# Adding the second bias of a feed-forward block on VectorE instead of TensorE, in a one-core training step

## The chip, the cores and the metric

The kernel runs on one core of one Trainium2 chip. The metric is device time in microseconds (us) of one execution; shorter is better. A core has five engines that run their own instruction streams: TensorE (PE in the profile; PEld is its weight load), VectorE (DVE), ScalarE (ACT), GpSimd (POOL) and SyncE (SP). SP, ACT and POOL issue DMA transfers from queues. Engines wait for each other by semaphores, and each works through its own stream in order.

## The reference

The reference is one transformer layer, forward and backward, on 2048 tokens of width 512 in bf16. The forward part is cut to what matters here:

```
def _B_ref(x, w1, b1, w2, b2):
    h = jnp.einsum("bsd,df->bsf", x, w1) + b1
    h = _gelu(h)
    return jnp.einsum("bsf,fd->bsd", h, w2) + b2

h  = x + _A_ref(_layernorm(x), A_wqkv, A_wo)        # sliding, dilated attention of 32 heads
h2 = h + _B_ref(_layernorm(h), B_w1, B_b1, B_w2, B_b2)
```

with F = 1792 hidden features. The outputs are h2 and the gradients of x, wqkv, wo, w1, b1, w2 and b2 for a given gradient of h2. The change concerns the term b2 in h2. It is one row of 512 numbers, added to each of the 2048 tokens.

## The kernel before, in words

The tokens are cut into NC = 4 chunks of CH = 512; a chunk is TPC = 4 token tiles of P = 128 rows. The kernel has three stages.

In the first stage, to about 150 us, `p1_round` does layer norm, the projections and the attention chunk by chunk. Its step `p1_d` leaves the residual h of a chunk in `h_all[c]`, a bf16 tile of 128 x 4 x 512 that stays on chip.

The second stage, the feed-forward block with its gradient, reaches to about 380 us. Two generators are interleaved by hand. `p2_h(c)` makes hidden activations of a chunk in four blocks of features: matmuls into `ps_h` (L583), two ACT evictions to `xb` and `xa` (L584, L585), a sigmoid on ACT (L590), and eight VectorE operations (L588 to L596) that end in `gt`, the gelu, and `dt`, its derivative. `p2_rest(c)` then does, for each of four token tiles, the product with w2 into `ps_f2` (shown in the profile as ps_f): 14 matmuls (L615), one matmul of a row of ones with the row `b2row` (L616), and one with the identity that adds the residual (L617). ACT copies the sum to `h2s` (L619) and stores it (L620). After that come the gradient products `ps_gg` (L628, multiplied into `dt` by VectorE at L630) and `ps_gl2` (L639), then the layer norm's gradient. While chunk c is in `p2_rest`, chunk c + 1 is in `p2_h`.

PSUM tiles rotate: `ps_h` has four buffers, `ps_f2` shares two with other tiles. `xb` and `xa` have two buffers each.

In these two stages a scheduler sets each engine's order of instructions from the program's dependences; the order of the code is only where it starts from. At the start of the second stage SP issues transposing loads of w2 and w1 (`w2T`, `w1T`) and of the gradient (`goT`), and transposes of `gt` and `dt` through `tst`, with POOL storing the results.

The third stage, from about 380 us, has its order written out by hand (`tc.manual_schedule()`): attention gradients on VectorE with weight gradients filled in on TensorE.

Of the kernel before, what the change touches and what calls it, by code (L numbers as in the profile page):

```python
# [10 lines left out]
P = 128  # L11
BF16 = mybir.dt.bfloat16
F32 = mybir.dt.float32
ACT = mybir.ActivationFunctionType
ALU = mybir.AluOpType
# [12 lines left out]
def _ap(apobj, dims, off=0):  # L28
    return bass.AP(tensor=apobj.tensor, offset=apobj.offset + off, ap=[list(d) for d in dims])
# [7 lines left out]
def kernel(  # L37
# [21 lines left out]
    V, A, T, G, SY = nc.vector, nc.scalar, nc.tensor, nc.gpsimd, nc.sync  # L59
# [4 lines left out]
    S, D = xf.shape  # L64
# [4 lines left out]
    TPC = CH // P  # L69
# [16 lines left out]
    def LP(name, side="left"):  # L86
        p = pool(name, 1, side)
        pools.append(p)
        return p

    const = LP("const")
# [8 lines left out]
    def Y(name):  # L100
        return psY.tile([P, 512], F32, name=name, tag="y")

    def TT(name):
        return psT.tile([P, 1024], BF16, name=name, tag="t")
# [9 lines left out]
    ind8 = const.tile([P, 8], BF16, name="ind8")  # L114
    Emat = const.tile([P, 4, 32], BF16, name="Emat")
    mk = const.tile([16, 2, 4, 32], BF16, name="mk")
    ones_row = const.tile([1, P], BF16, name="ones_row")
    ones_col = const.tile([P, 1], BF16, name="ones_col")
    mhalf = const.tile([P, TPC], F32, name="mhalf")
    zrow = const.tile([18, D], BF16, name="zrow")  # L120
    rowi = const.tile([P, 2], mybir.dt.uint32, name="rowi")
    V.memset(ones_row[:], 1.0)
    V.memset(mhalf[:], -0.5)
    V.memset(zrow[:], 0.0)
    rstd1 = const.tile([P, NT], F32, name="rstd1")
    rstd2 = const.tile([P, NT], F32, name="rstd2")
    b1b = const.tile([FT, P], BF16, name="b1b")
    b2row = const.tile([1, D], BF16, name="b2row")
    b1c = const.tile([P, FT], F32, name="b1c")
    gb1p = const.tile([P, FT, NC], F32, name="gb1p")  # L130

# [22 lines left out]
    def load_rows(t, src, c):  # L154
        SY.dma_start(out=t[:], in_=src[c * CH:(c + 1) * CH, :].rearrange("(j p) d -> p j d", p=P))
# [168 lines left out]
    h_all = []  # L324

    def p1_ln(c):
        xp, xg = ((wff, "w20"), (wff, "w28"), (early, "xt"), (late, "xt"))[c]
        xt = xp.tile([P, TPC, D], BF16, name="xt", tag=xg, bufs=1)
        load_rows(xt, xf, c)
        if c == 0:  # L330
            for i in range(3):
                o = (1, 0, 2)[i] * D
                SY.dma_start(out=wqkv[:, :, o:o + D], in_=A_wqkv[:, o:o + D].rearrange("(a p) j -> p a j", p=P))
        ln1 = early.tile([P, TPC, D], BF16, name="ln1", tag="ln1", bufs=2)
        layernorm(early, xt, rstd1, c, ln1)
        store_rows(ln1_d, c, ln1)
        ln1T = early.tile([P, DC, CH], BF16, name="ln1T", tag="ln1T", bufs=2)
        to_fm(ln1, ln1T)
        st_[c].update(xt=xt, ln1T=ln1T)
# [24 lines left out]
    def p1_v(c):  # L364
        vt = early.tile([P, 4, PAD + CH], BF16, name="vt", tag="vt", bufs=1)
        p1_proj(c, 2, vt, PAD)
        to_tm_store(early, vt, PAD, v_d, c, True)
        G.dma_start(out=vf_d[:, :, PAD + c * CH:PAD + (c + 1) * CH], in_=vt[:, :, PAD:PAD + CH])

    def p1_tm(c):  # L370
        to_tm_store(early, st_[c]["kt"], PAD, k_d, c, True)
        to_tm_store(early, st_[c]["qt"], 0, q_d, c, False)

    def p1_dots(c):
        d = st_[c]
        d["L"] = [X("ps_L") for _ in range(2)]
        dots(late, d["qt"], d["kt"], d["L"], c == 0)
# [57 lines left out]
    def p1_d(c):  # L435
        d = st_[c]
        oT, xt = d["oT"], d["xt"]
        ht = htile(f"h{c}")
        for j in range(TPC):
            ps = X("ps_wo")  # L440
            for k in range(DC):
                T.matmul(ps[:], lhsT=oT[:, k, j * P:(j + 1) * P], rhs=wo[:, k, :], start=(k == 0), stop=False)
            T.matmul(ps[:], lhsT=ident[:], rhs=xt[:, j, :], start=False, stop=True)
            A.copy(out=ht[:, j, :], in_=ps[:])
        h_all.append(ht)
        ln2 = late.tile([P, TPC, D], BF16, name="ln2", tag="ln2", bufs=1)
        layernorm(late, ht, rstd2, c, ln2)
        store_rows(ln2_d, c, ln2)
        d["ln2"] = ln2

    def p1_d2(c):
        to_fm(st_[c]["ln2"], ln2T[c])
# [34 lines left out]
    def p1_round(c):  # L487
        if c + 2 < NC:
            p1_ln(c + 2)
        if c == 0:  # L490
            for (d_t, r) in ((v_d[0], 0), (k_d[0], 0), (q_d[NC - 1], CH), (go_d[NC - 1], CH)):
                SY.dma_start(out=d_t[r:r + RPAD, :], in_=zrow[:])
            SY.dma_start(out=b1b[:], in_=B_b1.rearrange("(f p) -> f p", p=P))
            SY.dma_start(out=b2row[:], in_=B_b2.rearrange("(a n) -> a n", a=1))
        if c + 1 < NC:
            p1_dots(c + 1)
        if c > 0:
            p1_d(c - 1)
        if c == NC - 2:
            p1_v(c + 1)  # L500
        if c > 0:
            p1_d2(c - 1)
        if c + 2 < NC:
            p1_qk(c + 2)
        if c + 1 < NC:
            p1_sm1(c + 1)
        p1_o(c, 0)
        if c == NC - 1:
            return
        if c < NC - 2:  # L510
            p1_v(c + 1)
        p1_sm2(c + 1)
        p1_o(c, 1)
        p1_tm(c + 1)
        if c == 1:
            w2.extend(wparts(wff, "w2", W3, True))
            for a_, b_, t_ in w2:
                G.dma_start(out=t_[:], in_=B_w2[a_ * P:b_ * P, :].rearrange("(a p) d -> p a d", p=P))
        if c == 0:
            pb = TT("pb1")  # L520
            T.transpose(pb[:, 0:FT], b1b[:], ident[0:FT, 0:FT])
            V.tensor_copy(out=b1c[:], in_=pb[:, 0:FT])
# [14 lines left out]
    def load_wT(name, src):  # L537
# [3 lines left out]
    NS = 5  # L541
    SA = 2
    FFT = dict(goT=([P, DC, CH], 1), tst=([P, 16, P], 3), gout=([P, TPC, D], 1), ln2r=([P, TPC, D], 1),
               h2s=([P, D], 2), gyr=([P, D], 2), junk=([P, D], 1), u=([P, D], 2), 
               xb=([P, 4, PAD + CH], 2), xa=([P, 2, 4, 512], 2))

    ffp = {}
# [1 line left out]
    def ft(tag, name=None):  # L549
        shp, nb = FFT[tag]  # L550
        pl = ffA if tag in ("xb", "xa", "tst") else ffp["B"]
        return pl.tile(shp, BF16, name=name or tag, tag=tag, bufs=nb)
# [49 lines left out]
    def p2_rest(c):  # L602
        d = ps2[c]
        gts, dts = d["g"], d["d"]
        goT = goT0.pop() if c == 0 else ft("goT")
        if c > 0:
            SY.dma_start_transpose(out=goT[:], in_=gof[c * CH:(c + 1) * CH, :])
        gout = ft("gout")
        load_rows(gout, gof, c)
        ln2 = ft("ln2r")  # L610
        load_rows(ln2, ln2_d, c)
        for j in range(TPC):
            ps = psT.tile([P, 512], F32, name="ps_f2", tag="t")
            for f in range(FT):
                T.matmul(ps[:], lhsT=gts[f // 4][:, f % 4, j * P:(j + 1) * P], rhs=wrow(w2, f), start=(f == 0), stop=False)  # L615
            T.matmul(ps[:], lhsT=ones_row[:], rhs=b2row[:], start=False, stop=False)  # L616
            T.matmul(ps[:], lhsT=ident[:], rhs=h_all[c][:, j, :], start=False, stop=True)  # L617
            h2s = ft("h2s")
            A.copy(out=h2s[:], in_=ps[:])  # L619
            A.dma_start(out=h2f[c * CH + j * P:c * CH + (j + 1) * P, :], in_=h2s[:])  # L620
            yield
        for bi, (f0, f1) in enumerate(FB):
            for fp in range(f0, f1, 2):
                for i in range(2):
                    f = fp + i
                    ps = Y("ps_gg")
                    for dc in range(DC):
                        T.matmul(ps[:], lhsT=wcol(w2T, dc, f), rhs=goT[:, dc, :], start=(dc == 0), stop=(dc == DC - 1))  # L628
                    dsl = dts[bi][:, f - f0, :]
                    V.tensor_tensor_reduce(out=dsl, in0=ps[:], in1=dsl, scale=1.0, scalar=0.0,  # L630
                                           op0=ALU.mult, op1=ALU.add, accum_out=gb1p[:, f, c:c + 1])
                yield
            tok_store(dts[bi], f0, f1, ghT_d, c)
        gh = htile(f"gh{c}")
        gh_all[c] = gh
        for j in range(TPC):
            ps = psT.tile([P, 512], F32, name="ps_gl2", tag="t")
            for f in range(FT):
                T.matmul(ps[:], lhsT=dts[f // 4][:, f % 4, j * P:(j + 1) * P], rhs=wrow(w1T, f),  # L639
                         start=(f == 0), stop=(f == FT - 1))  # L640
            t = c * TPC + j
            ln_bwd(ffp["B"], ps[:], ln2[:, j, :], rstd2[:, t:t + 1], gout[:, j, :], gh[:, j, :])
            yield
# [82 lines left out]
    w1T = wparts(wfb, "w1T", W4, True)  # L726
    for a_, b_, t_ in w2T:
        SY.dma_start_transpose(out=t_[:], in_=B_w2[a_ * P:b_ * P, :])
    goT0 = [ft("goT")]
    SY.dma_start_transpose(out=goT0[0][:], in_=gof[0:CH, :])  # L730
    for a_, b_, t_ in w1T:
# [506 lines left out]
```

## Time and profile before

| | before |
|---|---|
| time, median of 5 runs | 666.92 us (664.36 to 672.56) |
| profiled execution: time | 665.72 us |
| profiled execution: span of the engines | 663.8 us |
| TensorE busy | 609.6 us, 3948 matmuls |
| VectorE busy | 512.9 us, 758 instructions |
| ACT busy | 367.4 us, 570 instructions |
| granted TensorE clock, mean | 0.992 |

The span is the time from the first to the last instruction of the profiled execution; the time around it is 1.9 us more. Busy time is the sum over an engine's instructions, overlaps counted once. In a timeline the first two numbers are start and duration in us; a bracket at the end tells how long the engine sat idle before, and what ended the wait. In a table of groups, the numbers behind the bar are busy us, mean ns of one, and idle us before them. L616 is line 616 of the kernel before.

### The profile page before, as it was taken

Reading aid. Unit: us, or ns where it says so; the run is one execution under the profiler, and the core shown is the slowest. Engines: PE = TensorE matmul, PEld = TensorE weight load, DVE = VectorE, ACT = ScalarE, POOL = GpSimd, SP = SyncE. Lnnn points to the kernel's source line nnn. Section 1 sums busy time; section 2 is a strip of 40 time slices with the busy share of each in tenths; the row PEclk is TensorE's granted clock in tenths of the full one; section 3 lists DMA queues with packets and bytes.
Section 4 is the critical chain, followed back from the end, with each engine's and each line's share of the span. In section 5 each row is a group of like instructions: output and inputs, shape, how many; then the busy total and the mean of one; then the engine's idle time right before and its main releaser. Section 6 shows DMA issues by size and latency. Waiting matters only on the chain. (4 is left out here: it accounts for less than half of the span.)

```text
span 663.8 us, 10258 instructions
## 1 busy us (share of the span) xinstructions
PE 609.6 (92%) x3948; PEld 285.5 (43%) x3948; DVE 512.9 (77%) x758; ACT 367.4 (55%) x570; POOL 161.1 (24%) x183
## 2 busy tenths in 40 slices
PE   3888989877899999999999899999999999989997
PEld 1343434332444344444344434434456566433443
DVE  7989989969879869859839797987987898296400
ACT  2588877788583645556331362863494356464311
POOL 3341635431001110110100234430323134030100
PEclk9999999898899999999999999999999999999999
DMA  8583848744999997987995989996899689979141
GB/s 257 193 301 119 295 138 305 225 153 105 241 223 274 238 219 170 219 223 180 257 252 162 247 315 349 368 321 234 281 403 327 218 283 356 299 247 319 50 158 48
DMA packets 147806, 158.87 MB, mean 239 GB/s; under 512 B 94461, under 2 KB 132398, under 8 KB 141102
## 3 DMA queue, kind: packets, MB, share of 16 engines
q1 hardware_dynamic: 120078, 69.58, 40.2%
q0 software_dynamic: 15376, 77.63, 34.0%
q10 hardware_dynamic: 12304, 11.01, 5.2%
q8 instruction: 31, 0.51, 0.3%
q14 instruction: 17, 0.14, 0.1%
HBM read 87.63 MB, written 48.03 MB: 204 GB/s over the span
## 5 line engine op out<-in xcount | busy, mean ns | idle before, releaser
L1021 DVE TENSOR_TENSOR prb<-R,cf 128x2048 bf16<-128x2048 bf16 x96 | 110.8, 1218 | 11.3 <-DMA R<-go_d,rowi 4.2
L188 ACT ACTIVATE gyr<-ps_gl,rstd 128x512 bf16<-128x512 f32 x32 | 21.9, 687 | 77.9 <-PE ps_gl L1084 32.0
L583 PE MATMUL ps_h<-ln2T,w 128*128 128x512 bf16 x224 | 56.9, 384 | 1.4 <-ACT xa L585 1.0
L913 PE MATMUL ps_gw<-gwm,ln_r 128*128 128x256 bf16 x448 | 53.1, 273 | 2.0 <-ACT gwst L832 1.0
L628 PE MATMUL ps_gg<-goT,w2T 128*128 128x512 bf16 x224 | 54.6, 378 | 0.3 <-DVE gb1p L630 0.3
L639 PE MATMUL ps_gl<-w1T,dt 128*128 128x512 bf16 x224 | 52.3, 379 | 1.6 <-ACT gyr L188 1.3
L905 PE MATMUL ps_gw<-gout_r,gwm 128*128 128x512 bf16 x224 | 53.1, 380 | 0.0
L615 PE MATMUL ps_f<-w,gt 128*128 128x512 bf16 x224 | 51.5, 379 | 0.4 <-DVE gt L591 0.4
L913 PEld LDWEIGHTS <-ln_r 128*128 128x128 bf16 x448 | 42.5, 98 | 13.7 <-issue 6.5
L659 DVE TENSOR_TENSOR pr<-got,vw 128x4096 bf16<-128x4096 bf16 x16 | 36.3, 2289 | 15.0 <-ACT got L656 11.4
L584 ACT ACTIVATE xb<-ps_h,b1c 128x512 bf16<-128x512 f32 x56 | 38.6, 697 | 16.7 <-DVE xa L595 10.7
L345 PE MATMUL ps_qkv<-ln1T,wqkv 128*128 128x512 bf16 x192 | 46.9, 386 | 0.7 <-ACT ln1T L167 0.6
L630 DVE CUSTOM_DVE_ANT_0 dt<-ps_gg,dt 128x512 bf16<-128x512 f32 x56 | 37.7, 685 | 11.2 <-PE ps_gg L628 11.2
L933 PE MATMUL ps_gwq<-gqh,ln_r 128*128 128x512 bf16 x192 | 42.6, 379 | 0.7 <-ACT gwst L832 0.7
L568 POOL DMA_DIRECT2D gT_d<-tst x16 | 12.1, 757 | 127.1 <-DMA tst<-gt 125.2
L585 ACT ACTIVATE xa<-ps_h,b1c 128x512 bf16<-128x512 f32 x56 | 38.7, 702 | 7.0 <-DVE dt L596 7.0
L266 DVE TENSOR_TENSOR prb<-R,cf 128x2048 bf16<-128x2048 bf16 x32 | 37.6, 1210 | 4.3 <-DMA R<-v_d,rowi 3.3
L1031 ACT ACTIVATE gks<-ps_band 128x512 bf16<-128x512 f32 x32 | 19.0, 598 | 36.3 <-PE ps_band L1029 31.7
L236 DVE TENSOR_TENSOR pr<-qt,kt 128x4096 bf16<-128x4096 bf16 x16 | 36.1, 2285 | 2.1 <-PE ps_band L271 1.1
L590 ACT ACTIVATE xa<-xa 128x2048 bf16<-128x2048 bf16 (+1 forms) x16 | 27.1, 1701 | 13.8 <-DVE xa L589 13.6
L639 PEld LDWEIGHTS <-dt 128*128 128x128 bf16 x224 | 21.4, 98 | 30.2 <-issue 3.0
L217 ACT COPY tmst<-ptm 128x1024 bf16<-128x1024 bf16 x32 | 31.2, 1019 | 4.5 <-PE ptm L214 2.6
(186 smaller groups left out, 1140.5 us busy)
## 6 DMA issues: line engine op xcount, KB each, us to landing
gwm<-ghT_d SPq DMA_DIRECT2D x7, 1024.0 KB
gT_d<-tst POOLq DMA_DIRECT2D x12, 512.0 KB
ghT_d<-tst POOLq DMA_DIRECT2D x12, 512.0 KB, 4.8
gwm<-gT_d SPq DMA_DIRECT2D x6, 1024.0 KB
out_dram<-gwst ACTq DMA_DIRECT2D x22, 256.0 KB
ln_d<-ln POOLq DMA_DIRECT2D x8, 512.0 KB, 5.7
vw<-vf_d SPq DMA_DIRECT2D x4, 528.0 KB
xt<-in_A_x_dram SPq DMA_DIRECT2D x4, 512.0 KB
```

Source lines behind the costliest of these rows:

```text
L345: T.matmul(ps[:], lhsT=wqkv[:, dc, sel * D + g * P:sel * D + (g + 1) * P], rhs=st_[c]["ln1T"][:, dc, :], start=(dc == 0), stop=(dc == DC - 1))
L583: T.matmul(ps[:], lhsT=wcol(w1, dc, f), rhs=ln2T[c][:, dc, :], start=(dc == 0), stop=(dc == DC - 1))
L584: A.activation(out=xb[:, f - f0, :], in_=ps[:], func=ACT.Identity, bias=b1c[:, f:f + 1])
L585: A.activation(out=x2[:, f - f0, :], in_=ps[:], func=ACT.Square, bias=b1c[:, f:f + 1])
L615: T.matmul(ps[:], lhsT=gts[f // 4][:, f % 4, j * P:(j + 1) * P], rhs=wrow(w2, f), start=(f == 0), stop=False)
L628: T.matmul(ps[:], lhsT=wcol(w2T, dc, f), rhs=goT[:, dc, :], start=(dc == 0), stop=(dc == DC - 1))
L630: V.tensor_tensor_reduce(out=dsl, in0=ps[:], in1=dsl, scale=1.0, scalar=0.0, op0=ALU.mult, op1=ALU.add, accum_out=gb1p[:, f, c:c + 1])
L639: T.matmul(ps[:], lhsT=dts[f // 4][:, f % 4, j * P:(j + 1) * P], rhs=wrow(w1T, f), start=(f == 0), stop=(f == FT - 1))
L905: yield from mm_pair("ps_gw2", lambda ps, o, u, i, t, k: T.matmul(ps[:], lhsT=g_[:, o, i * HN + t, :], rhs=gout_r[i][:, t, :], **k), MM, w ...
L913: yield from mm_pair("ps_gw1", lambda ps, o, u, i, t, k: T.matmul(ps[:, 256 * u:256 * u + 256].rearrange("p (a f) -> p a f", a=2), lhsT=ln ...
L933: yield from mm_pair("ps_gwq", lambda ps, o, u, i, t, k: T.matmul(ps[:], lhsT=ln1_r[i][:, t, (2 * d2 + o) * P:(2 * d2 + o + 1) * P], rhs=h ...
L1021: V.tensor_tensor(out=pr[:, 4 * hf:4 * hf + 4].rearrange("p j (d h) -> p j d h", h=H), in0=R[:, o:o + 4, :].rearrange("p j (d h) -> p j d ...
```

## The change

The row of ones and `b2row` go, with their memset and load, and so does the one-row matmul of every token tile. In their place b2 is loaded once to all 128 partitions (`b2b`, on ACT's DMA queue, emitted behind the transposing loads of w2), and `p2_rest` adds it in place to all four token tiles of the chunk's residual by one VectorE operation, ahead of the products with w2. `b2b` takes 1 KB per partition in the second stage's pool.

```diff
-    ones_row = const.tile([1, P], BF16, name="ones_row")
...
-    V.memset(ones_row[:], 1.0)
...
-    b2row = const.tile([1, D], BF16, name="b2row")
...
-            SY.dma_start(out=b2row[:], in_=B_b2.rearrange("(a n) -> a n", a=1))
...
-               h2s=([P, D], 2), gyr=([P, D], 2), junk=([P, D], 1), u=([P, D], 2), 
+               h2s=([P, D], 2), b2b=([P, D], 1), gyr=([P, D], 2), junk=([P, D], 1), u=([P, D], 2), 
...
         load_rows(ln2, ln2_d, c)
+        V.tensor_tensor(out=h_all[c][:], in0=h_all[c][:], in1=b2b[:].unsqueeze(1).to_broadcast([P, TPC, D]), op=ALU.add)
         for j in range(TPC):
             ps = psT.tile([P, 512], F32, name="ps_f2", tag="t")
             for f in range(FT):
                 T.matmul(ps[:], lhsT=gts[f // 4][:, f % 4, j * P:(j + 1) * P], rhs=wrow(w2, f), start=(f == 0), stop=False)
-            T.matmul(ps[:], lhsT=ones_row[:], rhs=b2row[:], start=False, stop=False)
             T.matmul(ps[:], lhsT=ident[:], rhs=h_all[c][:, j, :], start=False, stop=True)
...
         SY.dma_start_transpose(out=t_[:], in_=B_w2[a_ * P:b_ * P, :])
+    b2b = ft("b2b")
+    A.dma_start(out=b2b[:], in_=_ap(B_b2, [[0, P], [1, D]]))
     goT0 = [ft("goT")]
```

## The prediction

> **What bounds the kernel now.** I read the page's busy shares first, then busy time by stretch cut at the four b2 places, then the timelines of three engines around the first of these, since all that the change adds lands there.
>
> ```profile
> PE 609.6 (92%) x3948; PEld 285.5 (43%) x3948; DVE 512.9 (77%) x758; ACT 367.4 (55%) x570; POOL 161.1 (24%) x183
> ```
>
> TensorE leads, VectorE follows at 77%. An average over stages says too little, so here are stretches of the feed-forward stage. Columns: stretch, its length, busy us and instructions of PE, PEld, DVE, ACT, POOL, then granted clock, DMA share, GB/s.
>
> ```profile
> 164.80:168.10 3.30, 0.72 (x5) 0.11 (x2) 2.59 (x6) 1.76 (x4) 1.47 (x2) 1.00 1.00 209
> 168.20:171.50 3.30, 3.30 (x19) 2.13 (x20) 3.27 (x7) 1.93 (x3) 0.76 (x1) 0.50 1.14 216
> 172.20:187.00 14.80, 14.80 (x67) 5.97 (x65) 9.96 (x13) 8.90 (x13) 0.00 (x0) 1.00 1.12 260
> 187.00:230.00 43.00, 41.22 (x185) 17.56 (x184) 38.66 (x76) 26.84 (x45) 6.12 (x8) 1.00 1.09 242
> 230.00:242.00 12.00, 12.00 (x54) 4.90 (x53) 9.58 (x12) 4.41 (x6) 1.42 (x2) 1.00 1.09 257
> 242.00:281.00 39.00, 38.93 (x178) 17.02 (x177) 32.87 (x69) 23.47 (x41) 4.52 (x6) 1.00 0.87 190
> ```
>
> From 172 on TensorE is never out of work for long: 178 matmuls in 39 us is one per 0.219 us, and neighbours of one shape start 0.216 us apart in the trace. So a matmul taken out here shortens the stage, unless its place is taken by a wait. VectorE is the near second in 187 to 230 (38.7 of 43 us). The first two lines show a second thing: a stretch in which TensorE was 22% busy is followed by one at half clock.
>
> **What goes.** The 16 one-row matmuls, four per chunk:
>
> ```profile
> L616 PE MATMUL ps_f<-b2row,ones_row 1*128 1x512 bf16 x16 | 6.1, 384 | 0.0
> ```
>
> Durations overlap on this engine, so I count from start to start (timeline of PE, start and duration first):
>
> ```profile
> 179.61 3.19 PE L615 MATMUL ps_f<-w,gt 128*128 128x512 bf16 x14
> 182.73 0.38 PE L616 MATMUL ps_f<-b2row,ones_row 1*128 1x512 bf16 x1
> 183.05 0.39 PE L617 MATMUL ps_f<-h,ident 128*128 128x512 bf16 x1
> 183.27 3.19 PE L615 MATMUL ps_f<-w,gt 128*128 128x512 bf16 x14
> ```
>
> One group takes 183.27 - 179.61 = 3.66 us. Fourteen plus one matmuls at 0.216 are 3.24. So the one-row matmul costs 0.42, not 0.216: single starts put 0.311 ahead of it and 0.317 behind it, where 0.216 would stand without it (the identity matmul L443 after L442 shows 0.216). That is 0.311 + 0.317 - 0.216 = 0.412 each, 6.6 us for 16, of which 1.65 per chunk. [...] The row has the changed weight shape in it, so I take 6.6. Also gone are a memset of one row and a 1 KB load at 10 us, both beside other work: nothing.
>
> **What comes.** One load of b2 to all 128 partitions (128 KB) on ACT's queue, and four adds of 128x2048 bf16 on VectorE. In the built program's order the scheduler puts the load between two sigmoids at about 172 to 174 us, and all four adds, those of chunks 1 to 3 too, among VectorE's work at the end of chunk 0's and start of chunk 1's activation. So chunks 1 to 3 lose four matmuls each and get nothing: 12 x 0.412 = **4.9 us** off a full TensorE. The whole cost stands at chunk 0.
>
> An add is priced by L593, same size and type: 1.22 us, 1.14 from start to start, so 4.6 us. A broadcast operand does not change that: L1021 (128x2048 with one) takes 1218 ns. VectorE there, before:
>
> ```profile
> 173.91 1.83 DVE L591 TENSOR_TENSOR gt<-xa,xb 128x2048 bf16<-128x2048 bf16 x2 [2.06 <-ACT xa L590]
> 175.65 1.22 DVE L593 TENSOR_TENSOR xa<-xa,gt 128x2048 bf16<-128x2048 bf16 x1
> ...
> 181.32 0.69 DVE L596 TENSOR_TENSOR dt<-xa 128x1024 bf16<-128x1024 bf16 x1
> 185.07 0.69 DVE L588 TENSOR_SCALAR xa<-xa 128x2048 bf16<-128x2048 bf16 x1 [3.06 <-ACT xa L585]
> ...
> 189.00 1.23 DVE L591 TENSOR_TENSOR gt<-xa,xb 128x2048 bf16<-128x2048 bf16 x1 [1.37 <-ACT xa L590]
> ```
>
> Its holes of 3.06 and 1.37 us are where the adds go. I walk the new order with these durations. gt 173.9 to 175.05, L593 to 176.2, L594 to 176.8, the second gt to 177.4, L595 to 178.6, its short twin to 179.1, dt to 180.3, L594 to 180.65, **add of h0 to 181.8**, L595 to 182.4, add of h1 to 183.5, dt to 184.2. L588 may follow at once, since ACT's evictions come sooner (below), then add of h2 to 186.0, L589 to 187.1, L592 to 187.8, add of h3 to 188.9. The sigmoid between runs 187.2 to 189.1, so the next gt starts at 189.1, against 189.00. VectorE comes out 0.1 to 0.8 us late (one product of L630 stands behind where it stood).
>
> TensorE is where it hurts. In the new order the first two ps_f groups run as one, 28 matmuls without their last, then one ps_h, then both identity matmuls, which read h0 and so wait for the add. The 28 take 172.3 to 178.4. The ps_h needs a PSUM slot that ACT frees with its first xa: four xb from 178.6 (when L595 is done with their buffer) at 0.577 apart, then xa, done at 181.6. The identity matmuls start at 181.8. **A hole of some 3.3 us on TensorE**, where before it had none. Behind it stand seven ps_h (to 183.6); groups 3 and 4 of ps_f, which wait for the h2s copies that ACT does after its four xa (first at 183.3, done 183.8); and eight ps_h: 183.9 + 2 x 3.24 + 8 x 0.216 = 192.1 for the first ps_gg. Before it started at 190.39. So TensorE is 1.7 us late there, with its four saved matmuls already in it. In 187 to 230 it idled 43.0 - 41.2 = 1.8 us on VectorE and ACT; VectorE is hardly late, so part of this takes the lag up: 0 to 1.7 remain, I take 1.0.
>
> **Two unknown costs.** First the load. It must land by 180.65. No row shows it; near rows are the h2s stores of the same 128 KB on the same queue among the same transposes: by the landing semaphores 3.1 to 3.9 us after issue. The slowest near row is the 512 KB store ln_d at 7.5. Issued at 172.3 to 174, it lands by 176 to 178 at the near price: nothing; at the far one up to 181.5, a loss of 0.9. I take nothing, by the row of equal size. The program has no wait ahead of it that is still open, so ACT behind it loses only the issue, 0.35 us, ahead of a sigmoid that has over a microsecond of slack now. On SP the order gains only that a gout load goes one transpose sooner. One h2s store now waits for w1T's first transpose (landed at 188.4 before; ACT comes to it at 189.6): nothing.
>
> [...] The rows agree: gaps of 4.0 us (to 151.75) and 2.55 us (to 167.79) were each followed by 3.4 us at 0.50, one of 1.6 us (to 569.8) was not. [...] Ends 0 and 1.7; I take 1.0.
>
> **Sum.** -4.9 (chunks 1 to 3) + 1.0 (chunk 0, net of its own 1.65) + 1.0 (clock) = -2.9 us. The stages behind the feed-forward one follow it, with TensorE 267.6 of 284 us busy, and shift with it. Profiled execution: span 663.8, time 665.72, so 662.8. The median of the runs shown is 1.2 above that execution, so **664.0** as a median. The runs spread over 664.4 to 672.6, so 1% is about what can be told from no change here.
>
> **Rivals.**
> 1. *All 16 pay.* The hole is shorter than I think and swallowed by the 1.8 us of idling in 187 to 230, and the clock holds: -6.6, median 660.3. For it: VectorE has 4.4 us of holes for 4.6 us of adds. Against: two separate waits end at 181.6 and 181.8.
> 2. *The adds sit on the engine that sets the pace (slower).* In 187 to 230 VectorE is 90% busy; if its holes close (evictions are not sooner, so L588 stays near 185 with two adds still to come), all 4.6 us reach the first ps_gg products, the clock drops for 1.7, and the shorter ps_f groups of chunks 1 to 3 only wait longer for gt: +6.3, median 673.2. It decides once holes near 185 and 188 fall under about 1 us. Against: chunk 2's group starts with no wait on gt, chunks 1 and 3 wait 0.3 to 0.4.
> 3. *b2 lands late*, 7.5 us after issue: 0.9 more, and longer at half clock: median 665.6.
>
> **How the numbers follow.** The forecast 0.62, rival 1 0.14, rival 2 0.16, rival 3 0.08. The forecast's own range is 662.0 to 665.4 by the two ends of lag and clock, 661 to 667 with the scatter of a median. Faster by over 1% is under 660.3: half of rival 1 and a tail of the forecast, 0.14. Slower by over 1% is over 673.6: half of rival 2 and tails of the others, 0.15. Within 1%: 0.71. The range 659.5 to 671 takes in rivals 1 and 3 and reaches toward 2.
>
> **What would show it.** Right: the ps_f groups of chunks 1 to 3 3.24 us apart, not 3.66; four adds of 1.2 us between 180 and 189; a TensorE hole near 178 to 182 ended by ACT xa or the add; a half-clock interval right after; the first ps_gg near 192, then by 345 a lead of 2 to 4 us. Wrong: groups still 3.5 or more apart; the hole absent or over 5 us; an add that waits on the load; a stage end later than before.

## The result: no gain, and a lead that was there at 375 us

| | before | after |
|---|---|---|
| median | 666.92 us (79 runs) | 668.17 us (42 runs) |
| profiled execution: time, span | 665.72, 663.8 us | 667.56, 665.3 us |
| ratio after to before, 95% interval | | 1.0014 [1.0000, 1.0029] |

The forecast was 664.0, so 0.4% faster; the kernel came out the same or 0.1% slower. A ratio here leaves out slow executions, those over 1.5% above the fastest of their kernel. The page of the changed kernel, busy shares:

```profile
PE 607.6 (91%) x3932; PEld 286.3 (43%) x3932; DVE 518.6 (78%) x761; ACT 366.9 (55%) x570; POOL 151.9 (23%) x183
```

The 16 matmuls are gone, and VectorE is 5.7 us busier. To see where time went, I matched the instructions of the two profiled executions one by one and took the median shift of TensorE's starts, after minus before:

| stretch of before, us | 140 | 192 | 225 | 240 | 292 | 340 to 375 | 400 on |
|---|---|---|---|---|---|---|---|
| shift, us | +2.15 | +2.95 | +1.64 | +0.3 | -0.64 | -2.33 | +1.3, then to the end +1.6 |

The first 2.15 us come ahead of everything that the change touches in the second stage: up to 140 us this execution ran 3.4 us (from 24.3) and 6.8 us (from 130.1) at half clock (granted 0.50), that of before only 3.4 us (from 120.4). It is this execution's own: in e3_hold and e5_pool below, which differ from the changed kernel only in the third stage, the same shift is -0.7 and 0.8. From 160 to 375 us the changed kernel then **gains 4.5 us**. Between 380 and 395 it loses 3.7 us at one place, the beginning of the third stage. That loss is the matter of this study.

First the second stage, where the change was made. TensorE around the first b2 place (timeline of the changed kernel; its line numbers are 2 to 4 lower, the tiles' names are the same):

```profile
175.75 4.91 PE L612 MATMUL ps_f<-w,gt 128*128 128x512 bf16 x22
183.31 0.38 PE L579 MATMUL ps_h<-ln2T,w 128*128 128x512 bf16 x1 [2.65 <-ACT xa L581]
183.52 0.59 PE L613 MATMUL ps_f<-h,ident 128*128 128x512 bf16 x2
183.95 1.67 PE L579 MATMUL ps_h<-ln2T,w 128*128 128x512 bf16 x7
185.52 3.18 PE L612 MATMUL ps_f<-w,gt 128*128 128x512 bf16 x14
188.54 0.38 PE L613 MATMUL ps_f<-h,ident 128*128 128x512 bf16 x1
188.75 3.19 PE L612 MATMUL ps_f<-w,gt 128*128 128x512 bf16 x14
```

The hole of the prediction is there, 2.65 us long and ended by ACT's xa. Groups are 188.75 - 185.52 = 3.23 us apart, not 3.66. VectorE at the same time:

```profile
182.16 1.22 DVE L608 TENSOR_TENSOR h<-h,b2b 128x2048 bf16<-128x2048 bf16 x1
...
183.89 1.22 DVE L608 TENSOR_TENSOR h<-h,b2b 128x2048 bf16<-128x2048 bf16 x1
...
186.23 1.22 DVE L608 TENSOR_TENSOR h<-h,b2b 128x2048 bf16<-128x2048 bf16 x1
...
189.11 1.22 DVE L608 TENSOR_TENSOR h<-h,b2b 128x2048 bf16<-128x2048 bf16 x1
190.69 1.23 DVE L587 TENSOR_TENSOR gt<-xa,xb 128x2048 bf16<-128x2048 bf16 x1 [0.37 <-ACT xa L586]
```

All four adds stand in one stretch of 8 us, none with a wait on the load, and the next gt is late by 190.69 - 189.00 = 1.7 us, less than the 2.15 us by which the stage was entered late.

Now the beginning of the third stage. VectorE's first product there (timelines of before, then of the changed kernel):

```profile
382.04 9.17 DVE L1021 TENSOR_TENSOR prb<-R,cf 128x2048 bf16<-128x2048 bf16 x8 [2.27 <-DMA R<-k_d,rowi]
```

```profile
383.31 6.90 DVE L1019 TENSOR_TENSOR prb<-R,cf 128x2048 bf16<-128x2048 bf16 x6 [5.87 <-DMA R<-k_d,rowi]
```

VectorE was ready 2.3 us earlier (377.44 against 379.77) and began 1.3 us later. Both times the wait ends with the first indirect gather, `R<-k_d`, which POOL issues. The issues on POOL's and SP's queues then, in the order of time (start and duration of the issuing instruction, not of the transfer), before:

```profile
375.07 1.05 POOL L228 DMA_INDIRECT R<-k_d,rowi  x1 [0.31 <-issue]
...
376.62 0.55 SPq L886 DMA_DIRECT2D vw<-vf_d  x1
377.21 0.68 SPq L754 DMA_DIRECT2D gwm<-gT_d  x1
377.94 0.44 SPq L155 DMA_DIRECT2D ln1r<-ln_d  x1
```

and the same lines of the changed kernel:

```profile
366.92 1.23 SPq L884 DMA_DIRECT2D vw<-vf_d  x1
...
372.53 1.16 POOL L225 DMA_INDIRECT R<-k_d,rowi  x1 [0.31 <-DMA vw<-vf_d]
...
372.99 0.34 SPq L752 DMA_DIRECT2D gwm<-gT_d  x1
373.37 0.44 SPq L152 DMA_DIRECT2D ln1r<-ln_d  x1
```

The gather goes out 2.5 us earlier, as it should with that lead. But vw goes out 9.7 us earlier, and gwm (1 MB), with ln1r (512 KB) behind it, now follows the gather by 0.5 us instead of 2.1. By the landing semaphores the gather took 375.07 to 382.02, 6.95 us, before, and 372.53 to 383.28, **10.75 us**, after.

Why vw moves is seen in the two built programs: before, vw waits for TensorE and for two DMAs; after, for one DMA alone. In SP's order gwm and ln1r stand behind vw (376.62, 377.21 and 377.94 before; 366.92, 372.99 and 373.37 after), so they move too. Nothing in the change names vw. But the constants lose 1,280 bytes per partition (row of ones, `b2row`), so the tiles of the third stage lie 1,280 bytes lower. In the kernel before, vw begins at byte 192,896 of each partition and reaches into the old `dt`, so that it waits for the last ps_gl matmul that reads that tile, near 376 us. In the changed kernel it begins at 191,616 and ends short of `dt`, over the old `xa` and `gt`, which were read long before. The 1,024 bytes that the second stage's pool gains do not matter for this: in e7_pad below they stay, and vw waits for TensorE again.

The DMA packets of the two traces show what the gather then meets. In the first 8 us behind its issue SP's queue moved 0.14 MB before and 1.04 MB after; the gather's first packet came 1.74 and 3.16 us after the issue. TensorE ran 3.4 us at half clock from 386.1 in the changed kernel, but its shift there, +1.37, is VectorE's delay of 1.3 and no more.

### The profile page after: what moved, and what is told of

Same layout as the page of the kernel before. It is cut to its first block, busy times and chain, and to the rows that moved or that the text cites. A ratio compares the mean times of both kernels' runs of the same rounds, so it can differ in the third digit from the quotient of the medians.

```text
span 665.3 us, 10230 instructions
## 1 busy us (share of the span) xinstructions
PE 607.6 (91%) x3932; PEld 286.3 (43%) x3932; DVE 518.6 (78%) x761; ACT 366.9 (55%) x570; POOL 151.9 (23%) x183
## 5 line engine op out<-in xcount | busy, mean ns | idle before, releaser
L342 PE MATMUL ps_qkv<-ln1T,wqkv 128*128 128x512 bf16 x192 | 48.3, 394 | 0.7 <-DMA go_d<-zrow 0.6
L1027 PE MATMUL ps_band<-prb,S 128*32 128x512 bf16 x384 | 30.8, 389 | 4.4 <-DVE prb L1019 4.3
```

What stands on the lines that cost most here:

```text
L342: T.matmul(ps[:], lhsT=wqkv[:, dc, sel * D + g * P:sel * D + (g + 1) * P], rhs=st_[c]["ln1T"][:, dc, :], start=(dc == 0), stop=(dc == DC - 1))
```

## The experiments

Theory A: the changed addresses let the third stage's loads out early, and these slow the gather that VectorE waits for. Rival B: the boundary takes the lead back whatever the loads do. Rival C, later: chunk 0's hole costs the end nothing. All ratios are against the kernel before on the same chip, median 668.2 to 668.3 us there; that of the changed kernel is against the 666.92 us measured with it.

**The changed kernel with b2 in the constants (e1_layout), a first try at the old addresses.**

```diff
+    ones_row = const.tile([1, P], BF16, name="ones_row")
...
+    b2b = const.tile([P, D], BF16, name="b2b")
...
-    b2b = ft("b2b")
```

> The change with the on-chip addresses of the kernel before: b2b lies where b2row lay in the constant pool, the row of ones stays as a filler, and the second stage's pool no longer grows by 1 KB. Theory A (the lead of the second stage is lost at the third stage's start: the new addresses freed SP's load of vw from a wait on TensorE, so the 1 MB load gwm and ln1r come level with the first gather of k rows and stretch it from 6.9 to 10.8 us): vw waits for TensorE again, the gather takes about 7 us, VectorE's first product of the third stage idles about 2 us on it and not 5.9, and the time is 3.5 to 4.5 us under the kernel before, ratio 0.993 to 0.995. Theory B (the lead is lost for another reason, such as a slower clock at that point or a third stage that keeps its own pace): ratio about 1.001 as for the change.

Measured: 0.9995 [0.9965, 1.0024], not what A expected. The edit did more than planned: the scheduler also put instructions of TensorE, VectorE and ACT in another order from about 140 us on, and only 1.6 us were gained from 160 to 375. vw did wait for TensorE again, but POOL came to the gather late, so that vw and gwm followed it by 0.44 and 1.0 us and the first product idled 4.80 us. Too many things moved; it decides nothing.

**The kernel before with the new addresses (e2_before_layout).** The 16 matmuls stay; their two rows lie where other tiles already are or in the second stage's pool.

```diff
-    ones_row = const.tile([1, P], BF16, name="ones_row")
-    b2row = const.tile([1, D], BF16, name="b2row")
...
+            V.memset(b1b[0:1, :], 1.0)
...
-            T.matmul(ps[:], lhsT=ones_row[:], rhs=b2row[:], start=False, stop=False)
+            T.matmul(ps[:], lhsT=b1b[0:1, :], rhs=b2b[0:1, :], start=False, stop=False)
...
+    b2b = ft("b2b")
+    A.dma_start(out=b2b[0:1, :], in_=B_b2.rearrange("(a n) -> a n", a=1))
```

> The kernel before with the addresses of the change: all 16 one-row matmuls stay, but the row of ones lies in b1b's first row and b2's row in a tile of the second stage's pool, so that the constants shrink and the pool grows as in the change. Theory A: vw no longer waits for TensorE, the first gather of k rows takes 10 to 11 us in place of 6.9, VectorE idles about 6 us on it in place of 2.3, and the time is 3 to 4 us over the kernel before, ratio 1.004 to 1.006. Theory B: ratio 1.000 within 0.002.

Measured: **1.0068 [1.0041, 1.0096]**. With no add at all, the addresses cost 0.7%. POOL and SP, then VectorE, at the boundary of this kernel:

```profile
373.98 1.23 POOL L225 DMA_INDIRECT R<-k_d,rowi  x1 [0.31 <-DMA vw<-vf_d]
...
374.50 0.34 SPq L753 DMA_DIRECT2D gwm<-gT_d  x1
374.89 0.43 SPq L152 DMA_DIRECT2D ln1r<-ln_d  x1
```

```profile
385.15 8.04 DVE L1020 TENSOR_TENSOR prb<-R,cf 128x2048 bf16<-128x2048 bf16 x7 [6.20 <-DMA R<-k_d,rowi]
```

It is the picture of the changed kernel: gwm 0.5 us behind the gather, gather 11.1 us, 6.20 us idle. The scheduler moved a few instructions in the second stage too, but its shift against before is -0.7 us at 160 and -0.8 from 229 to 380, so they cost nothing; here 3.9 us are lost.

**Holding gwm and ln1r back in SP's order, to behind the first q band (e3_hold on the changed kernel, e4_before_hold on the one before).**

```diff
-    tiles.append(load_t(gT_d, 1))
...
-    load_ln1(0)
...
+                if c == 0 and k == 0:
+                    tiles.append(load_t(gT_d, 1))
+                    load_ln1(0)
```

> The change as it is, but the loads gwm (second) and ln1r of the third stage stand behind the first band of work in SP's order, after the stores of go rows. Addresses as in the change. Theory A: the gather has the transfer engines nearly to itself (vw has landed by then), takes about 7 us, VectorE starts the third stage 3 to 4 us sooner after the last gh, ratio to the kernel before 0.992 to 0.995. Theory B: ratio about 1.001 as for the change.

> The kernel before with the same two loads held back, as a control. Theory A: there the gather was already ahead of both loads, so it gains little: ratio 0.998 to 1.001. Theory B, in the form that the order of these loads is worth several us of itself whatever the change: ratio 0.993 to 0.995.

Measured: 1.0005 [0.9974, 1.0037] and 0.9994 [0.9968, 1.0020]. A's 0.992 to 0.995 for e3_hold was missed. In both kernels the times fell in two groups (for e3_hold 10 runs of 663.5 to 669.5 us and 12 of 673 to 681), and a ratio of such a mixture says little. The profiled execution of e3_hold is of the first group, 663.48 us: there the gather took 7.9 us, VectorE idled 3.03 us, and the end came 2.3 us earlier than in that of before. So the boundary moved as A says. But the hold is no clean test, since gwm can now come too late. The profiled execution of e4_before_hold, 675.39 us, is of the second group and shows that:

```profile
411.94 3.82 PE L904 MATMUL ps_gw<-gout_r,gwm 128*128 128x512 bf16 x10 [9.00 <-DMA gwm<-gT_d]
```

It had kept a lead of 1.3 us up to this wait and was 9.4 us late behind it, with 10.2 us at half clock from 404.8. Why some executions met the wait and others did not was not tested.

**The changed kernel with 1,280 bytes of filler (e7_pad).** This is the clean form of the first try: only addresses move, those of the third stage's tiles back to where they were before (b2b keeps its place in the second stage's pool), and every instruction of TensorE, VectorE, ScalarE and POOL keeps the order of the changed kernel, a memset of the filler apart.

```diff
+    pad = const.tile([1, 640], BF16, name="pad")
+    V.memset(pad[:], 0.0)
```

> The changed kernel with 1,280 bytes of filler per partition in the constants, so that the load of vw waits for TensorE again as in the kernel before; every instruction of TensorE, VectorE, ScalarE and POOL stands in the order of the changed kernel, apart from one small memset. Theory A (the early loads of the third stage slow the first gather): vw goes out some 1.5 us after the first gather, the gather takes 7 to 8 us and not 10.8, VectorE's first prb idles 2 to 3 us and not 5.9, and the lead of some 3 us over the kernel before survives the boundary: 0.993 to 0.996. Rival B (the third stage's start is set by something else that does not follow the lead, whatever the loads do): the shift goes back to about 0 at the boundary all the same, 0.999 to 1.002.

Measured: **0.9961 [0.9938, 0.9984]**, median 665.09. POOL and SP, then VectorE, of its profile:

```profile
372.00 1.28 POOL L227 DMA_INDIRECT R<-k_d,rowi  x1 [0.31 <-ACT c L189]
...
373.86 0.55 SPq L886 DMA_DIRECT2D vw<-vf_d  x1
374.46 0.69 SPq L754 DMA_DIRECT2D gwm<-gT_d  x1
375.20 0.45 SPq L154 DMA_DIRECT2D ln1r<-ln_d  x1
```

```profile
379.42 9.17 DVE L1021 TENSOR_TENSOR prb<-R,cf 128x2048 bf16<-128x2048 bf16 x8 [2.40 <-DMA R<-k_d,rowi]
```

Loads 1.9 to 3.2 us behind the gather, gather 7.4 us, idle 2.40: those of before, only 2.6 us earlier. B falls. With e2_before_layout this makes a square, in which addresses and add are changed one at a time:

| ratio to before | addresses of before | addresses of the change |
|---|---|---|
| 16 matmuls | 1 | 1.0068 (e2_before_layout) |
| four adds | 0.9961 (e7_pad) | 1.0014 (after) |

By rows, the addresses cost 0.7% and 0.5%; by columns, the add saves 0.4% and 0.5%. The two effects add up and nearly cancel. The second row is the cleaner of the two, since only there the order of instructions is the same.

**gwm and ln1r on POOL's queue, behind both gathers (e5_pool on the changed kernel, e6_before_pool on the one before).** `load_t` loads gwm, `load_R` issues a gather, `G` is POOL.

```diff
-    tiles.append(load_t(gT_d, 1))
...
-    load_ln1(0)
     load_R()
     load_R()
+    tiles.append(load_t(gT_d, 1, G))
+    load_ln1(0, G)
```

> The changed kernel with the first gwm (1 MB) and ln1r (512 KB) loads of the third stage issued by POOL, directly behind the first two gathers, and no longer by SP ahead of them; vw (early, 367) stays on SP. Theory A: with the large loads behind both gathers on the same queue the first gather takes 7 to 8 us, the first prb idles 2 to 3 us, and the later loads are not as late as in the hold (gwm lands by 392), so that TensorE finds its tile: 0.993 to 0.996. Rival B: 0.999 to 1.002 with a first prb that idles 5 us or more.

> The control of the last one: the same move of gwm and ln1r to POOL's queue in the kernel before, where the gather took 6.95 us as it was. Theory A: nothing to gain, 0.998 to 1.001, gather about 7 us. Rival B: the same. If this one gains as much as the move gains in the changed kernel, the move is good by itself and says nothing about the change.

Measured: **0.9946 [0.9922, 0.9970]** and 1.0043 [1.0019, 1.0067]. In e5_pool vw still goes out early (367.9), the gather took 8.2 us and VectorE idled 3.14: so gwm and ln1r close behind the gather do most of the harm, not vw. What is left over the 6.95 to 7.4 us goes with the early vw: in e5_pool and e3_hold the store that stands ahead of the gather on POOL's queue sent its last packet 2.9 us behind the gather's issue, in before and e7_pad 1.0 us. The control missed its expectation: it was to be level and is slower. Its profile names the place, TensorE at the second gwm:

```profile
406.68 2.33 PE L904 MATMUL ps_gw<-gout_r,gwm 128*128 128x512 bf16 x10 [2.68 <-DMA gwm<-gT_d]
```

That 1 MB load went out at 395.17, in before at 395.41, but landed at 406.63 and not at 400.54: here POOL issued its second `R<-go_d` gather 6.3 us earlier (394.80 against 401.14), and the load ran beside it. That fits the slowing of the gather with the parts exchanged, here 11.5 us for the load and not 5.1, though no run tested it alone. That the move gains in one kernel and loses in the other also shows that it isn't a gain of its own.

**The kernel before without the 16 matmuls and without any add (e8_nob2).** b2 is left out of h2, the tiles stay.

```diff
-            T.matmul(ps[:], lhsT=ones_row[:], rhs=b2row[:], start=False, stop=False)
```

> The kernel before without the 16 one-row matmuls and without any addition in their place (b2 is left out of h2); the tiles all stay, so the addresses and SP's waits are those of before. This measures TensorE's saving by itself, without the order of chunk 0 and without the new addresses. By the step of the prediction, 16 x 0.412 = 6.6 us less in the second stage. Theory A: vw waits for TensorE as before and follows the lead, so most of it reaches the end: 0.990 to 0.994. Rival B (the boundary to the third stage takes the lead back whatever the loads do): 0.996 to 1.000.

Measured: 0.9895 [0.9858, 0.9931], 7.0 us of 668.3, in an interval of 4.6 to 9.5. The step's 6.6 us lie in it; 16 times the 0.216 us that stand between the starts of neighbours of one shape, 3.5 us, do not. The saving rests on these times: the profiled execution, 666.01 us, is the second slowest of the eleven (median 661.89). In it TensorE once waited 4.43 us for gt (to 231.66), with 6.8 us at half clock from 229.9; behind that, the rest of chunks 1 to 3 gained 4.2 us.

**b2 added as soon as h is there (e9_early).** b2b lies in the constants in place of `b2row`, with 256 bytes of filler, and SP loads it in the first stage.

```diff
+    b2b = const.tile([P, D], BF16, name="b2b")
...
+            SY.dma_start(out=b2b[:], in_=_ap(B_b2, [[0, P], [1, D]]))
...
+    def add_b2(c):
+        V.tensor_tensor(out=h_all[c][:], in0=h_all[c][:], in1=b2b[:].unsqueeze(1).to_broadcast([P, TPC, D]), op=ALU.add)
...
+        if c > 0:
+            add_b2(c)
...
+    add_b2(0)
     hn = p2_h(0)
```

> The addition stays, but b2b lies in the constants, is loaded in the first stage and is added to each h as soon as h is there (in the first stage for chunks 0 to 2), so that chunk 0's chain on VectorE is free of it; constants and feed-forward pool have the size of the kernel before, and vw waits for TensorE. It separates what chunk 0's hole costs from what the third stage took. Theory A (16 x 0.412 saved, chunk 0's hole worth 1 to 3 us, the loads worth the rest): no hole at 178 to 182, gather 7 to 8 us, near the kernel without b2 (0.9895) less up to four additions of 1.22 us where VectorE sets the pace of the first stage: 0.990 to 0.995. Rival C (chunk 0's hole costs nothing that reaches the end, the loads are all of it): as with the filler, 0.996 or more.

Measured: **0.9907 [0.9872, 0.9942]**, median 662.03: faster than both kernels, and near the one without b2. TensorE at the first b2 place, without a hole, and the boundary:

```profile
174.33 0.38 PE L621 MATMUL ps_f<-h,ident 128*128 128x512 bf16 x1
174.54 1.67 PE L620 MATMUL ps_f<-w,gt 128*128 128x512 bf16 x7
176.06 0.38 PE L621 MATMUL ps_f<-h,ident 128*128 128x512 bf16 x1
176.27 3.19 PE L620 MATMUL ps_f<-w,gt 128*128 128x512 bf16 x14
```

```profile
374.38 9.17 DVE L1026 TENSOR_TENSOR prb<-R,cf 128x2048 bf16<-128x2048 bf16 x8 [2.19 <-DMA R<-k_d,rowi]
```

C expected 0.996 or more, but the time alone does not settle it. Against e7_pad the ratio is 0.5% less, about 3.6 us (the two intervals just touch). In the profiled executions e9_early is 2.2 us further ahead already at 162 us (shift -3.02 against -0.77), ahead of the hole's place: the other order of the scheduler closed a hole of 4.0 us that TensorE has in before (to 151.75). From 162 to 225 us, where e7_pad has the hole and its half clock, e9_early gains 2.4 us more (0.6 gained against 1.8 lost). These 2.4 us are what the traces give the hole with its half clock, so C falls by them.

## Why the prediction was wrong, point by point

- **The price of a one-row matmul, 0.412 us: right.** Groups stand 3.23 us apart where 3.66 stood; chunks 2 and 3 gained 1.7 us each (-0.64 less +1.05, -2.33 less -0.64). The chunk 1 groups gained 1.3 (0.3 less 1.64), of which 0.7 went back at once, near 248, where VectorE has waited 0.65 us for ACT's xa and TensorE then waits 0.49 us for VectorE. Chunks 1 to 3 gave 4.0 us in after and 3.8 in e7_pad, against 4.9 forecast.
- **Chunk 0: mechanism right, too dear.** Forecast a hole of 3.3 us and a net lag of 1.0; the hole was 2.65 us and the first ps_gg, counted from the stage's own late entry, 3.33 - 2.15 = 1.2 us late (forecast 1.7). By 225 the lag was taken up: 2.15 to 1.64, a net gain of 0.5.
- **The clock, 0 or 1.7: both ends occurred.** No run shows the 1.0 us that the sum has for the clock, or a length of hole from which the clock drops; what the profiled executions show behind chunk 0's hole is 3.4 us at half clock or none. After the 2.65 us hole that of the changed kernel stayed at full clock, in e7_pad it did not; there TensorE idled 2.48 and, one matmul later, 1.13 us more. In e5_pool and e3_hold, with the same order, holes of 2.88 and 3.19 us were followed by 3.4 us at half clock. So of these four only that of the changed kernel kept its clock, with a hole of 2.65 us, while in before one of 2.55 us (to 167.79) was followed by 3.4 us at half clock. Windows of the changed kernel, then of e7_pad (stretch, length, PE, PEld, DVE, ACT, POOL, granted clock, DMA share, GB/s):

```profile
180.70:183.30 2.60, 0.00 (x0) 0.00 (x0) 2.60 (x5) 2.60 (x6) 0.00 (x0) 1.00 1.13 250
183.30:186.70 3.40, 3.39 (x16) 1.54 (x16) 3.40 (x6) 2.91 (x6) 0.00 (x0) 1.00 1.09 241
```

```profile
175.60:182.10 6.50, 2.89 (x13) 1.17 (x12) 5.21 (x7) 4.74 (x8) 0.00 (x0) 1.00 1.18 228
182.10:185.50 3.40, 3.40 (x10) 1.21 (x8) 3.40 (x5) 2.35 (x5) 0.00 (x0) 0.50 1.03 243
```

  With the half clock the second stage gave 2.0 us (from -0.77 to -2.76, e7_pad), without it 4.5 (after). The forecast's terms give 2.2 and 3.9. Over all runs of a kernel the median granted clock was 0.989 to 0.991 before, 0.987 in e7_pad (hole alone), 0.985 in e2_before_layout (late gather alone) and 0.984 in the changed kernel. One stretch of 3.4 us at half clock lowers the mean by 3.4 / 2 / 665 = 0.0026, so by this estimate the changed kernel has about two such stretches more per execution; the forecast had one, that of the hole.
- **The load of b2 "lands by 176 to 178": wrong, and hidden by chance.** It went out at 172.12 and landed at 179.91, 7.8 us and not 3.9, above even the far end of 7.5; the first add stood at 182.16. The four stores of chunk 0 that the near price was read from took 3.2 to 3.9 us, but in the same trace one of chunk 1, of the same size on the same queue, took 7.0 (issued at 238.21). In e7_pad the load of b2 took 11.3 us, and rival 3's wait was there, at 1.3 us:

```profile
180.46 1.23 DVE L610 TENSOR_TENSOR h<-h,b2b 128x2048 bf16<-128x2048 bf16 x1 [1.29 <-DMA b2b<-in_B_b_dram]
```

- **The step that failed: "The stages behind the feed-forward one follow it … and shift with it."** It rested on TensorE's busy share there. But the third stage starts with VectorE waiting for a gather, and what moves beside that gather was changed by the addresses: 1.04 MB on SP's queue in its first 8 us, and not 0.14. I had read what each queue gets by the diff, and not the waits of the built program past the second stage; the missing wait of vw on TensorE stood in it. So the term that the prediction put at nothing was the start of the third stage: VectorE's idle time there grew from 2.27 to 5.87 us. The traces put 3.7 us at this place; by the square above the addresses cost 0.5 to 0.7%, 3.5 to 4.5 us.
- **Even with the loads in place the lead did not pass whole.** In e7_pad 2.76 us before the boundary became 1.59 at the end. The next gate is another gather, VectorE in before, then in e7_pad:

```profile
406.13 4.63 DVE L1021 TENSOR_TENSOR prb<-R,cf 128x2048 bf16<-128x2048 bf16 x4 [4.17 <-DMA R<-go_d,rowi]
```

```profile
404.92 4.63 DVE L1021 TENSOR_TENSOR prb<-R,cf 128x2048 bf16<-128x2048 bf16 x4 [5.59 <-DMA R<-go_d,rowi]
```

  VectorE came there 2.6 us earlier and started 1.2 us earlier. POOL issued that gather 2.9 us earlier (389.32 against 392.23), but it took 15.5 us to land and not 13.8; why was not tested.
- **Rivals.** The adds did not close VectorE's holes to the price of rival 2. What took the gain back was a mechanism that none of the three named; that the time still lies in the range given, 659.5 to 671, is no merit of the argument.

## What to carry to other kernels

A change that adds or drops a tile can move the addresses of others (by 1,280 bytes here), and with them which loads wait for which engine, also in stages that the diff does not touch: compare the waits of each load in both built programs to the end, and look for what becomes early as closely as for what becomes late. A wait that holds large loads back can be what keeps a critical gather fast: 7.4 us with it in e7_pad, 10.75 without it in the changed kernel. And when a lead vanishes at a stage's beginning, change addresses and work one at a time: two runs, one with filler and one with tiles moved, made here a square that no single comparison could have shown.

## What the runs showed of the hardware

In the profiled executions below an indirect gather into 128 x 5120 bf16 took 6.95 to 8.6 us where gwm went out 1.0 us or more behind it, and 10.75 to 11.1 us where gwm went out 0.5 us behind it on another queue. With what SP's queue moved in the first 8 us behind the gather's issue:

| kernel | gwm (1 MB) behind the gather, us | SP's queue, MB | gather, us |
|---|---|---|---|
| before | 2.1 | 0.14 | 6.95 |
| e7_pad | 2.5 | 0.13 | 7.4 |
| e1_layout | 1.0 | 0.72 | 8.6 |
| e2_before_layout | 0.5 | 1.07 | 11.1 |
| after | 0.5 | 1.04 | 10.75 |
| e5_pool (gwm on POOL's queue, behind both gathers) | 3.4 | 0.10 | 8.2 |
| e3_hold | 13.1 | 0.12 | 7.9 |

From before to after the gather became 3.8 us longer; how large loads close behind it do that, no run shows. And size alone did not tell the time of a small transfer: the load of 128 KB took 7.8 to 11.3 us among transposes (after, e7_pad), where the 16 stores of the same size on the same queue took 1.7 to 7.0 us in before.
